# A two-layer transformer kernel on one core: another opening, score banks of a group from different row bands, and another pace table

## The chip, the core and the metric

The kernel runs on one core of a Trainium2 chip. The core has TensorE (PE; its weight loads are listed as PEld), VectorE (DVE), ScalarE (ACT), GpSimd (POOL) and SyncE (SP, which issues the DMAs). The metric is device time in microseconds of one execution.

## The reference

```python
x = A_x                                   # 2048 tokens, 448 features, bf16
x = x + attention(layernorm(x), wqkv, wo) # 16 heads of 28, softmax over all 2048 keys
x = x + mlp(layernorm(x), w1, b1, w2, b2) # relu(h)**2, hidden size 1792
x = x + attention(layernorm(x), wqkv, wo) # the same weights again
x = x + mlp(layernorm(x), w1, b1, w2, b2)
```

With `attention`: `softmax(q k^T / sqrt(28)) v`, all heads side by side, times `wo`. The layernorm has no weights. The exponential of 2 x 16 x 2048 x 2048 scores is the largest single piece of work.

## The kernel before, in words

**Units.** A head takes 32 rows of TensorE (28 used), so four heads, a group, stand side by side in K and Q as four row bands (`hh`, 0 to 3) of 32 rows; there are 4 groups. A unit is one head's scores of 512 columns, that is one PSUM bank: two key tiles of 128 against a block of 256 queries (four key tiles against 128 queries for the last blocks). Each layer has 1024 units. A pass is (layer, query block, group, range of key tiles); its units come as key step by key step, four heads each.

**Score groups.** `s_stream` takes the units three at a time, into one of two score buffers `sc` of three banks (matmuls at L978, one row band per unit, `tile_position`). `e_stream` has ScalarE compute the exponential of a whole score group in one instruction (L1003), three or two banks wide, into one of 12 buffers `pt`. Where it is two, VectorE takes the third bank (`a_unit`, `a_rest`): it computes the exponential as powers of two with a polynomial in three instructions (L1068, L1089, L1109), and POOL does a fourth (L1092). There are 683 score groups, numbered by `gi`. Which units VectorE takes is decided by `apart`: not if VectorE's load or backlog is over thresholds (`BUSY`, `TB`, `LOW`, `TB2`), unless `gi` stands in `FORCE`, and never if it stands in `SKIP`. `apart` may choose a unit of the next pass instead (`LAG`), and only there does it look for a row band that the group hasn't got yet. `LEAD` and `STOP` keep it out of the first 15 groups and the last 80 units.

**Other streams.** `p_stream` multiplies the probabilities by V (L1173) and copies or adds partial sums (L1199, L1201); `norm_pair` and `norm_turn` divide by the row sums; `chain` does the output projection, the second layernorm, the MLP (L693 for all dense matmuls) and, in layer 0, the layernorm and K, Q, V of layer 1 for that block. `first_block` does layernorm (L546, L551, L656, L608) and K, Q, V (L716, L712 or L710, L744) of each block of 256 tokens in layer 0, as the loads of x land. `heat` puts in matmuls with no use where TensorE's load is low, and a score group may be computed twice (`MORE`) for the same reason. `wprep` copies the projection weights into heads of 32 rows (L493 on ScalarE, L495 on VectorE).

**Order.** Everything is put in an order at build time by a planner. It keeps a clock for each engine and an expected duration for each operation, and issues next the stream whose operation can start first, by priority where two can. Most of the numbers at the top of the file are priorities, thresholds and expected durations of this planner; `PACE` overwrites them when the score group number reaches the key. The chip then executes the instructions of each engine strictly in the planned order.

**Opening.** Layer 0 can't wait until K exists for all tokens, so the first two query blocks go over the keys in pieces: `OPENING` lists (query block, first key tile, last key tile), and partial sums are kept between the pieces. In block 0, `GS0` says which groups of heads are projected together: `((0, 2), (2, 2))` is two groups at a time, first group and count. `GATE` holds back the layernorm of a block until a score group or a projection has been issued. `FIRSTS`, `VP`, `QP`, `VG`, `VG1`, `VP2` are priorities and gates of the first blocks and their V; `WQA` says from which head on the copies of wq go to VectorE.

The lines by which the order of the opening is set, and the choice of the units of a group:

```python
OPENING = ((0, 0, 2), (0, 2, 4), (1, 0, 4), (0, 4, 8), (1, 4, 8), (0, 8, 12), (0, 12, 16), (1, 8, 16))
GATE = (None, None, ('s', 2), ('Q', 0, 2, 0), ('s', 8), ('s', 10), ('s', 8), ('s', 14))
FIRSTS = (4, 1.5)
GS0 = ((0, 2), (2, 2))
...
js = ahead(3)
us = [units[j] for j in js]
```

Of the kernel before, what the change touches and what calls it, by code (L numbers as in the profile page):

```python
# [52 lines left out]
MARGIN = 1.5  # L53
# [9 lines left out]
ONE = 1  # L63
# [18 lines left out]
KEEP = 6  # L82
LAG = 12
LEAD = 15
LAST = 690
BUSY = 0.97
TB = 2.2
TB2 = 0.9
SPAN = 15
# [4 lines left out]
MORE = 1  # L94
# [3 lines left out]
LASTP = 3.2  # L98
HOLD = 6
HOLD1 = 7  # L100
SOON = 0
NHP = 2
THIRD = 1
NL = 0
# [14 lines left out]
TADD = 2  # L119
THALF = 0  # L120
CUTS = (0, 10, 16)
CH = 4.0
MMC = 0.46
EFIRST = 0
VGAP = 0.0
QP = 8.0
FORCE = (24, 30, 31, 58, 59, 129, 192, 193, 272, 289, 295, 320, 324, 326, 376, 384, 419, 425, 474, 475, 476, 479, 481,
        523, 525, 536, 537, 539, 553, 555, 557, 568, 570, 573, 579, 581, 582, 583, 600, 605)
SKIP = (57, 132, 133, 135, 195, 198, 199, 273, 278, 288, 292, 379, 381, 383, 385, 386, 390, 427, 429, 430, 472, 478,
        480, 485, 487, 521, 522, 543, 575, 603)  # L130
PACE = {
    0: {'ASIDE': 2.0, 'BUSY': 0.97, 'CH': 4.0, 'CHUNK': 2, 'C_PRIO': 1.6, 'EPRIO': 2.5, 'FAR': 9, 'HOLD': 6,
         'KEEP': 6, 'L1N': 5.6, 'LAG': 12, 'LASTP': 3.2, 'LEAD': 15, 'MARGIN': 1.5, 'NEAR': 6, 'PRE': 0.5,
         'QP': 8.0, 'SOON': 0, 'SPAN': 15, 'TB': 2.2, 'TB2': 0.9, 'V_AGE': 5, 'V_LAST': 2.5, 'V_LATE': 4.6,
         'V_PAST': 2},
    8: {'V_LATE': 3.5, 'EPRIO': 8},
    16: {'EPRIO': 2.5},
    40: {'LAG': 16},
    56: {'CHUNK': 1},
    72: {'EPRIO': 8, 'LEAD': 12, 'SOON': 1.0},  # L140
    96: {'LAG': 12, 'KEEP': 4},
    112: {'V_LAST': 3.5},
    120: {'BUSY': 0.995, 'ASIDE': 1.0},
    136: {'BUSY': 0.985, 'CHUNK': 3},
    144: {'BUSY': 0.995, 'CHUNK': 1},
    264: {'HOLD': 5},
    272: {'HOLD': 6, 'LAG': 8, 'TB': 2.6, 'V_LAST': 1.8},
    280: {'LAG': 12, 'TB': 2.2, 'V_LAST': 3.5, 'PRE': 0.8},
    288: {'PRE': 0.5},
    296: {'PRE': 0.3},  # L150
    320: {'C_PRIO': 2.6},
    328: {'CHUNK': 3},
    336: {'CHUNK': 1},
    344: {'EPRIO': 2.5, 'L1N': 5.0},
    360: {'SPAN': 11},
    376: {'LASTP': 2.6, 'SPAN': 15},
    384: {'TB': 3.0, 'TB2': 1.4},
    392: {'TB': 2.2, 'TB2': 0.9},
    400: {'MARGIN': -1, 'V_LATE': 4.0, 'SPAN': 20},
    408: {'C_PRIO': 1.6},  # L160
    416: {'FAR': 17, 'SOON': 0},
    432: {'LAG': 8},
    440: {'LAG': 12, 'CH': 5, 'EPRIO': 4},
    496: {'LASTP': 3.2},
    536: {'NEAR': 4},
    560: {'FAR': 9, 'QP': 5},
    576: {'V_PAST': 5, 'TB': 3.0},
    584: {'V_PAST': 0, 'TB': 2.2, 'CH': 3.3, 'V_AGE': 6},
    600: {'BUSY': 0.97, 'SOON': 1.0},
    608: {'BUSY': 0.995, 'SOON': 0},  # L170
    632: {'TB': 1.8, 'C_PRIO': 4.2},
    640: {'FAR': 17, 'CHUNK': 2},
    648: {'LAG': 5},
    656: {'LAG': 12},
}


# [134 lines left out]
def kernel(  # L312
# [43 lines left out]
    pl = Planner()  # L356
# [457 lines left out]

    for qb, lo, hi in OPENING:
        add_passes(0, [qb], (lo, hi))
# [10 lines left out]
    units = []  # L827
# [5 lines left out]
    ends_at = {pi: i for i, (pi, *_) in enumerate(units)}  # L833
# [4 lines left out]
    at = [0]  # L838

    taken = set()  # L840
# [24 lines left out]

    def apart(i, now, us, soon=SOON):

        if len(units) - i < STOP or not LEAD <= len(gbuf) <= LAST:
            return None
        l, qb = passes[units[i][0]][:2]  # L870
        if sum(r.when() is not None and r.when() <= now + soon for r in sets_of(units[i])) <= (0 if soon else pending[0]):
            return None
        j = i
        if i + LAG > ends_at[units[i][0]]:
            j = ends_at[units[i][0]] + 1
            while j in taken:
                j += 1
            if j >= len(units):
                return None
            rows = {u[3] for u in us}  # L880
# [24 lines left out]

    def needs(unit):
        pi, kb, r, hh = unit
        l, qb, g, *_ = passes[pi]
        t0, nt = blocks[l][qb]
        return [("K", l, g, kb + i) for i in range(r)] + [("Q", l, g, t0 + i) for i in range(nt)]  # L910

    def s_stream():
        while at[0] < len(units):
            gi = len(gbuf)
            globals().update(PACE.get(gi, {}))
            js = ahead(3)
            us = [units[j] for j in js]
            gbuf.append({"n": len(us)})

            def fn(e, gi=gi, us=us, js=js):  # L920
# [5 lines left out]
                def next_at(j):  # L926
                    at[0] = j
                    rest = ahead(1)
                    at[0] = rest[0] if rest else len(units)
                    return rest  # L930
                own, j = True, None
                if OWN3 and bank_free(o.start) and next_at(js[-1] + 1):
                    j = apart(at[0], o.start, us)
                if j is None and len(us) == 3 and THIRD:
                    own = False
                    next_at(js[1] + 1)
                    j = apart(at[0], o.start, us[:2], 0.0)
                if j is None:
                    next_at(js[-1] + 1)
                else:  # L940
                    if not own:
                        us, ks = us[:2], ks[:2]
                        gbuf[gi]["n"] = 2
                    us, ks = us + [units[j]], ks + [3]
                    taken.add(j)
# [3 lines left out]
                    next_at(at[0])  # L949
# [16 lines left out]
                again = 0  # L966
                if short > 0 and gi > 0:
                    last = ("e" in gbuf[gi - 1] and gbuf[gi - 1]["e"].end) or pl.clock["ACT"] + 1.35
                    again = max(0, min(MORE, int(min(o.room, last - LAT["PE"] - 0.05 - o.end) / 0.22)))
                o.more = 0.22 * again  # L970
                for i in list(range(4)) * (again + 1):
                    for k, (pi, kb, r, hh) in enumerate(us):
                        if i >= r:
# [3 lines left out]
                        rows = slice(DHP * hh, DHP * hh + DHP)  # L977
# [4 lines left out]
            o = gbuf[gi]["s"] = Op("PE", 0.234, fn,  # L982
                                   deps=list({d for u in us for d in needs(u)}), acq=R_sc, mode="row", sets=("s", gi))
# [492 lines left out]
```

## Time and profile before

| | us |
|---|---|
| three runs | 842.81, 844.40, 844.43 |
| median | 844.4 |
| the profiled execution: its own time | 842.93 |
| its span | 841.1 |
| ScalarE busy | 825.3 |
| VectorE busy | 795.8 |
| TensorE busy | 790.1 |
| first exponential starts | 10.63 |

The span runs from the first to the last instruction of the program; some 1.8 us of the execution lie around it. The granted TensorE clock is full speed throughout. A row of a group reads: line, engine, operation, output and input tiles, shapes, count, then busy us, mean ns of one, and the engine's idle time just before with what ended it. A row of a timeline reads: start us, length us, engine, line, operation, count, and in brackets the engine's idle time before it. Exponentials overlap at their ends, so that the mean duration of one is longer than the distance from start to start.

### The profile page before, as it was taken

What the parts mean: (1) busy time and instruction counts of PE and PEld (TensorE: products, weight loads), DVE (VectorE), ACT (ScalarE), POOL (GpSimd) and SP (SyncE); (2) the same over time, 40 slices, a digit from 0 to 9 for tenths busy, and PEclk for the clock granted to TensorE, in tenths of its full rate; (3) what the DMA queues carried; (4) which work ended last, traced back from release to release, by engine and by line L of the source; (5) the groups of instructions that cost most, each with busy time, mean ns of one, the idle gap of its engine ahead of it and who ended that gap; (6) DMA issues with size and microseconds to landing.
All of it is one profiled execution on the core that took longest, in us unless ns stands there. A gap on an engine that the chain in (4) does not pass through costs nothing.

```text
span 841.1 us, 27889 instructions
## 1 busy us (share of the span) xinstructions
PE 790.1 (94%) x11972; PEld 423.3 (50%) x11972; DVE 795.8 (95%) x1548; ACT 825.3 (98%) x699; POOL 220.3 (26%) x338
## 2 busy tenths in 40 slices
PE   8999999999999999999999999889999999999997
PEld 4455545454545554455554544444444544545655
DVE  7999999999999999999999999999999999999954
ACT  8999999999999999999999999999999999999994
POOL 3211222323232222322222223232324133232200
PEclk9999999999999999999999999999999999999999
DMA  9200100000000000000000000011100000000000
GB/s 251 68 3 2 29 17 15 15 15 16 15 2 16 15 15 16 14 3 15 2 3 2 2 3 2 15 28 28 34 8 20 21 20 26 13 21 15 21 14 13
DMA packets 32312, 17.93 MB, mean 21 GB/s; under 512 B 17786, under 2 KB 31739, under 8 KB 32188
## 3 DMA queue, kind: packets, MB, share of 16 engines
q1 hardware_dynamic: 32188, 16.16, 7.0%
q8 instruction: 93, 1.52, 0.8%
q14 instruction: 31, 0.25, 0.1%
HBM read 13.87 MB, written 2.06 MB: 19 GB/s over the span
## 4 chain that ended last, share of the span: by engine, by line
ACT 47%; PE 34%; DVE 10%; issue 8%; POOL 0%; DMA 0%; ACTq 0%; DVEq 0%; POOLq 0%
ACT pt L1003 47%; PE mt L693 14%; PE sc L978 12%; PE oT L1173 7%; DVE v_e L1089 1%; DVE v_i L1068 1%; PE sc L693 1%; PE mt L1425 1%; DVE K_sb L1068 1%; DVE r L1369 1%; DVE V_sb L1089 1%; DVE oTn L1300 0%; DVE V_sb L1068 0%; DVE pt L1109 0%; DVE x_sb L1309 0%
## 5 line engine op out<-in xcount | busy, mean ns | idle before, releaser
L1003 ACT ACTIVATE pt<-sc 128x1536 bf16<-128x1536 f32 (+1 forms) x683 | 814.6, 1469 | 2.0 <-PE sc L978 1.9
L978 PE MATMUL sc<-Q_sb,K_sb 32*128 32x256 bf16 (+1 forms) x5038 | 298.1, 265 | 40.8 <-ACT pt L1003 35.0
L978 PEld LDWEIGHTS <-K_sb 32*128 32x128 bf16 x5038 | 128.7, 92 | 217.0 <-issue 171.4
L1092 POOL TENSOR_SCALAR v_i<-v_i 128x512 int32<-128x512 int16 x129 | 96.3, 746 | 255.1 <-DVE v_e L1089 252.4
L1173 PE MATMUL oT<-pt,V_sb 128*32 128x256 bf16 (+1 forms) x4070 | 150.6, 268 | 1.1 <-DVE K_sb L608 0.8
L693 PE MATMUL mt<-xnT,w 128*128 128x256 bf16 (+1 forms) x912 | 120.3, 270 | 0.5 <-DVE xnT L608 0.3
L1173 PEld LDWEIGHTS <-V_sb 128*32 128x32 bf16 x4352 | 92.1, 96 | 45.7 <-issue 43.1
L693 PEld LDWEIGHTS <-w 128*128 128x128 bf16 x952 | 77.7, 98 | 36.4 <-issue 28.5
L1068 DVE TENSOR_SCALAR v_i<-sc 128x512 int32<-128x512 f32 x129 | 88.1, 685 | 4.2 <-PE sc L978 3.5
L1089 DVE SCALAR_TENSOR_TENSOR v_e<-v_i 128x512 f32<-128x512 uint16 x129 | 89.5, 704 | 0.2
L1092 POOL TENSOR_SCALAR K_sb<-K_sb 128x512 int32<-128x512 int16 x68 | 47.9, 704 | 131.8 <-DVE K_sb L1089 130.1
L1369 DVE TENSOR_SCALAR r<-mt 128x512 bf16<-128x512 f32 (+1 forms) x109 | 74.4, 683 | 4.2 <-PE mt L693 3.8
L693 PE MATMUL mt<-w,V_sb 128*128 128x448 bf16 x274 | 69.4, 355 | 0.0
L1092 POOL TENSOR_SCALAR V_sb<-V_sb 128x512 int32<-128x512 int16 x46 | 31.1, 676 | 104.8 <-DVE V_sb L1089 103.9
L1068 DVE TENSOR_SCALAR K_sb<-sc 128x512 int32<-128x512 f32 x68 | 46.5, 685 | 1.7 <-PE sc L978 1.3
L1089 DVE SCALAR_TENSOR_TENSOR K_sb<-K_sb 128x512 f32<-128x512 uint16 x68 | 46.1, 688 | 0.2
L573 POOL TENSOR_TENSOR ve<-mv,eps_t 128x2 f32<-128x2 f32 (+1 forms) x34 | 14.1, 416 | 114.6 <-DVE mv L551 114.2
L1309 DVE TENSOR_TENSOR x_sb<-x_sb,mt 128x448 bf16<-128x448 bf16 x61 | 37.2, 611 | 7.1 <-PE mt L693 7.1
L546 DVE BATCH_NORM_STATS2 st<-x_sb 128x6 f32<-128x448 bf16 x62 | 38.0, 616 | 0.9 <-DMA x_sb<-in_A_x_dram 0.7
L693 PEld LDWEIGHTS <-V_sb 128*128 128x128 bf16 x302 | 24.5, 97 | 25.4 <-issue 12.2
L1109 DVE SCALAR_TENSOR_TENSOR pt<-v_e,v_i 128x512 bf16<-128x512 f32 x52 | 35.7, 689 | 0.2 <-POOL v_i L1092 0.2
L1068 DVE TENSOR_SCALAR V_sb<-sc 128x512 int32<-128x512 f32 x46 | 31.5, 685 | 1.6 <-PE sc L978 1.6
(114 smaller groups left out, 857.4 us busy)
## 6 DMA issues: line engine op xcount, KB each, us to landing
rec<-scr SPq DMA_DIRECT2D x54, 128.0 KB
x_sb<-in_A_x_dram SPq DMA_DIRECT2D x8, 224.0 KB
out_dram<-x_sb SPq DMA_DIRECT2D x15, 112.0 KB
w<-in_B_w_dram SPq DMA_DIRECT2D x1, 1568.0 KB
w<-in_B_w_dram SPq DMA_DIRECT2D x1, 1344.0 KB
dn<-oT_sb SPq DMA_DIRECT2D x54, 4.0 KB
V_sb<-in_A_wqkv_dram SPq DMA_DIRECT2D x4, 168.0 KB
scr<-dn SPq DMA_DIRECT2D x27, 8.0 KB
```

The costliest lines, as they stand in the source:

```text
L546: nc.vector.bn_stats(out=box["st"][:, :], in_=x_sb[:, t0 + j, :] if src is None else src())
L573: nc.gpsimd.tensor_tensor(out=ve[:, a:b], in0=mv[0][:, a:b, 1], in1=eps_t[:, a:b], op=ALU.add)
L693: nc.tensor.matmul(box["t"][:, c0:c0 + n], lhsT=lhsT() if callable(lhsT) else lhsT, rhs=rhs, start=a, stop=b)
L978: nc.tensor.matmul(dst[k][:, i * nt * P:(i + 1) * nt * P], lhsT=K_sb[l][rows, g, (kb + i) * P:(kb + i + 1) * P], rhs=Q_sb[rows, g, t0 * P: ...
L1003: t = nc.scalar.activation(out=pt[:, 0:n], in_=gbuf[gi]["sc"][:, 0:n], func=AF.Exp, scale=float(np.log(2.0)) * 2.0 ** -FRAC)
L1068: t = nc.vector.tensor_scalar(out=box["i"], in0=two(src), scalar1=EXP_BIAS, scalar2=EXP_LOW, op0=ALU.add, op1=ALU.max)
L1089: nc.vector.scalar_tensor_tensor(out=box["h"], in0=box["f"], scalar=lin, in1=box["f"], op0=ALU.add, op1=ALU.mult)
L1092: (nc.vector if e == "DVE" else nc.gpsimd).tensor_scalar(out=box["e"], in0=box["n"], scalar1=2.0 ** 22, scalar2=EXP_BASE, op0=ALU.mult, op ...
L1109: nc.vector.scalar_tensor_tensor(out=box["two"](pd), in0=box["h"], scalar=low, in1=box["e"].bitcast(DT.float32), op0=ALU.add, op1=ALU.mult)
L1173: nc.tensor.matmul(box["t"][DHP * hh:DHP * hh + DHP, 0:n], lhsT=V_sb[l][:, kb + i, 4 * g + hh, :], rhs=p[:, c0:c0 + n], start=begin and kb ...
L1309: nc.vector.tensor_tensor(out=x_sb[:, tb, lo:hi], in0=x_sb[:, tb, lo:hi], in1=t[:, 0:hi - lo], op=ALU.add)
L1369: nc.vector.tensor_scalar(out=r[:, 0:w], in0=t[:, 0:w], scalar1=0.0, scalar2=None, op0=ALU.max)
```

## The change

The new version of the file does four things.

- In the opening, block 0 is projected by single groups of heads, two passes change places with two others, the gates, priorities and the place of V differ, the copies of wq all go to ScalarE (`WQA = 16`), and the statistics of block 1 wait for the transposed x of block 0 (`XT = 1`).
- `ahead` fills a group of three with units of different row bands: it looks up to `AHEADS` = 4 units further, takes a unit out of turn only if its K and Q are there already, and falls back to the next ones in turn. `use` keeps the list of units that were taken out of turn. In `apart` the search for another row band (`AHEADV` = 6) holds within a pass too.
- The planner expects 0.2 us more for a score group with a row band twice (`deep`).
- `FORCE`, `SKIP`, `PACE` and several defaults have new values.

```diff
-EPRIO = 2.5
+EPRIO = 4
-WQA = 8
+WQA = 16
-L0N = 7.0
+L0N = 5
-XT = 0
+XT = 1
-OPENING = ((0, 0, 2), (0, 2, 4), (1, 0, 4), (0, 4, 8), (1, 4, 8), (0, 8, 12), (0, 12, 16), (1, 8, 16))
+OPENING = ((0, 0, 2), (0, 2, 4), (1, 0, 4), (1, 4, 8), (0, 4, 8), (0, 8, 12), (1, 8, 16), (0, 12, 16))
-GATE = (None, None, ('s', 2), ('Q', 0, 2, 0), ('s', 8), ('s', 10), ('s', 8), ('s', 14))
+GATE = (None, None, ('Q', 0, 2, 0), ('Q', 0, 2, 0), None, None, ('s', 5), None)
-FIRST = 50
-V_FIRST = 9
+FIRST = 40
+V_FIRST = 7
+AHEADS = 4
+AHEADV = 6
-FIRSTS = (4, 1.5)
+FIRSTS = (4, 3)
-GS0 = ((0, 2), (2, 2))
+GS0 = ((0, 1), (1, 1), (2, 1), (3, 1))
-VP = 4.2
+VP = 8
-VG = 2
-VG1 = 5
-VP2 = 4.3
+VG = 3
+VG1 = 2
+VP2 = 3
-QP = 8.0
-FORCE = (24, 30, 31, 58, 59, 129, ...
-SKIP = (57, 132, 133, 135, 195, ...
+QP = 9
+FORCE = (21, 33, 34, 36, 74, 77, 79, 87, 109, 110, 130, 132, 157, 158, 159, 260, 416, 419, 448, 450, 451, 455, 536,
+        617, 620, 622, 623, 642, 643, 646)
+SKIP = (17, 20, 22, 24, 25, 26, 28, 31, 32, 35, 37, 39, 72, 73, 75, 78, 86, 131, 133, 134, 135, 155, 156, 258, 259,
+        417, 452, 454, 538, 540, 619, 621, 644, 647)
...
+    304: {'MORE': 3},
+    328: {'V_PAST': 5},
...
+    400: {'TB2': 2.2, 'MARGIN': 0.5, 'V_LAST': 3.5},
...
+    488: {'MORE': 1, 'BUSY': 1.01, 'V_LATE': 4.6},
+    552: {'MARGIN': 2.5, 'TB': 1.8},
...
-        j = i
-        if i + LAG > ends_at[units[i][0]]:
-            j = ends_at[units[i][0]] + 1
+        j, end = i, ends_at[units[i][0]] + 1
+        rows = {u[3] for u in us}
+        if i + LAG >= end:
+            j, end = end, len(units)
...
-            js = [k for k in range(j, j + 4) if k < len(units) and k not in taken and units[k][3] not in rows]
-            j = js[0] if js else j
+        js = [k for k in range(j, min(j + AHEADV, end)) if k not in taken and units[k][3] not in rows]
+        j = js[0] if js else j
...
     def ahead(n):
-        return [i for i in range(at[0], min(at[0] + n + len(taken), len(units))) if i not in taken][:n]
+        c = [i for i in range(at[0], min(at[0] + n + AHEADS + len(taken), len(units))) if i not in taken][:n + AHEADS]
+        out = []
+        for i in c:
+            if len(out) < n and units[i][3] not in {units[k][3] for k in out} and (i in c[:n] or all(pl.tok.get(d) is not None and pl.tok[d].end < pl.clock["PE"] for d in needs(units[i]))):
+                out.append(i)
+        return out + [i for i in c if i not in out][:n - len(out)]
+    def use(js):
+        taken.update(js)
+        while at[0] in taken:
+            taken.discard(at[0])
+            at[0] += 1
+        rest = [i for i in range(at[0], min(at[0] + 1 + len(taken), len(units))) if i not in taken]
+        return rest[0] if rest else len(units)
...
-                o.more = 0.22 * again
+                deep = max(sum(u[3] == w[3] for u in us) for w in us) - 1
+                o.more = 0.22 * again + 0.2 * deep * (again + 1)
```

More of the change, by code (lines that the diff above doesn't have):

```diff
@@ L100 @@
 HOLD1 = 7
-SOON = 0
+SOON = 1
 NHP = 2
@@ L125 @@
 VGAP = 0.0
-QP = 8.0
[L127 to L130, printed above, removed]
-PACE = {
[L132 to L142, printed above, removed]
-    120: {'BUSY': 0.995, 'ASIDE': 1.0},
[L144 to L174, printed above, removed]
@@ new lines @@
+QP = 9
[3 more added lines that the diff above has]
+        417, 452, 454, 538, 540, 619, 621, 644, 647)
+PACE = {
+    0: {'ASIDE': 2.0, 'BUSY': 0.97, 'CH': 4.0, 'C_PRIO': 1.6, 'EPRIO': 4, 'EV': 2.9, 'KEEP': 6, 'L0N': 5,
+         'L1N': 5.6, 'LAG': 12, 'MARGIN': 1.5, 'MORE': 1, 'NEAR': 2, 'QP': 9, 'SOON': 1, 'TB': 2.2, 'TB2':
+         0.9, 'V_AGE': 6, 'V_LAST': 2.5, 'V_LATE': 4.6, 'V_PAST': 2, 'V_PRIO': 8.5, 'V_WAIT': 5},
+    24: {'C_PRIO': 2.6},
+    32: {'C_PRIO': 1.6},
+    48: {'EPRIO': 1.5},
+    88: {'V_LATE': 4.0},
+    104: {'QP': 5},
+    112: {'QP': 9},
+    120: {'BUSY': 0.995, 'ASIDE': 1.0},
+    168: {'EV': 3.3, 'V_LAST': 1.8, 'V_WAIT': 3.5},
+    304: {'MORE': 3},
+    328: {'V_PAST': 5},
+    336: {'LAG': 5},
+    344: {'LAG': 12, 'EV': 1.5},
+    392: {'V_PAST': 2, 'V_LATE': 5.2},
+    400: {'TB2': 2.2, 'MARGIN': 0.5, 'V_LAST': 3.5},
+    416: {'MORE': 1, 'EPRIO': 4},
+    424: {'KEEP': 3, 'EV': 3.3},
+    432: {'V_PAST': 5, 'CH': 3.3},
+    440: {'MORE': 3, 'EPRIO': 2.5},
+    448: {'MORE': 1, 'EPRIO': 1.5, 'L1N': 5.8, 'KEEP': 6},
+    456: {'L1N': 5.6, 'KEEP': 3, 'EPRIO': 2.5},
+    480: {'MORE': 3},
+    488: {'MORE': 1, 'BUSY': 1.01, 'V_LATE': 4.6},
+    552: {'MARGIN': 2.5, 'TB': 1.8},
+    568: {'L0N': 8.4, 'V_LATE': 2.7},
+    576: {'L0N': 5, 'V_LATE': 4.6},
+    632: {'V_PAST': 0, 'V_PRIO': 3.5},
+    648: {'V_AGE': 3, 'SOON': 0},
+    656: {'V_AGE': 6, 'SOON': 1},
@@ L879, in apart @@
                 return None
-            rows = {u[3] for u in us}
-            js = [k for k in range(j, j + 4) if k < len(units) and k not in taken and units[k][3] not in rows]
-            j = js[0] if js else j
+        js = [k for k in range(j, min(j + AHEADV, end)) if k not in taken and units[k][3] not in rows]
+        j = js[0] if js else j
         if passes[units[j][0]][0] != passes[us[0][0]][0]:
@@ L924, in fn @@
                 ks = list(range(len(us)))
[L926 to L930, printed above, removed]
                 own, j = True, None
-                if OWN3 and bank_free(o.start) and next_at(js[-1] + 1):
-                    j = apart(at[0], o.start, us)
+                i = use(js[:2])
                 if j is None and len(us) == 3 and THIRD:
                     own = False
-                    next_at(js[1] + 1)
-                    j = apart(at[0], o.start, us[:2], 0.0)
+                    j = apart(i, o.start, us[:2], 0.0)
                 if j is None:
-                    next_at(js[-1] + 1)
+                    use(js[2:])
                 else:
@@ L944, in fn @@
                     us, ks = us + [units[j]], ks + [3]
-                    taken.add(j)
+                    use([j])
                     gbuf[gi]["in"] = not own and units[j][0] == us[0][0]
@@ L948, in fn @@
                     pending[0] += 1
-                    next_at(at[0])
                     if own:
```

2 lines of the change are left out of this document (1 added, 1 removed).

## The prediction

> **What bounds the kernel now.** I read the page's engine shares first, then the groups of instructions with shapes kept apart, then the busy time by stretches, then the opening in order of time.
>
> ```profile
> span 841.1 us, 27889 instructions
> ...
> PE 790.1 (94%) x11972; PEld 423.3 (50%) x11972; DVE 795.8 (95%) x1548; ACT 825.3 (98%) x699; POOL 220.3 (26%) x338
> ```
>
> Three engines are nearly full, and ScalarE (ACT) most of all. The next view says with what; behind the x stand the count, the busy us and the mean ns of one.
>
> ```profile
> L1003 ACT ACTIVATE pt<-sc 128x1536 bf16<-128x1536 f32 x439 | 644.6, 1621 | 1.9 <-PE sc L978 1.9
> L1003 ACT ACTIVATE pt<-sc 128x1024 bf16<-128x1024 f32 x244 | 278.6, 1195 | 0.2
> L1089 DVE SCALAR_TENSOR_TENSOR v_e<-v_i 128x512 f32<-128x512 uint16 x129 | 89.5, 704 | 0.2
> L1068 DVE TENSOR_SCALAR v_i<-sc 128x512 int32<-128x512 f32 x129 | 88.1, 685 | 4.2 <-PE sc L978 3.5
> L1109 DVE SCALAR_TENSOR_TENSOR pt<-v_e,v_i 128x512 bf16<-128x512 f32 x52 | 35.7, 689 | 0.2 <-POOL v_i L1092 0.2
> L1199 DVE COPY K_sb<-oT 128x256 f32<-128x256 f32 x20 | 8.4, 418 | 0.3 <-PE oT L1173 0.3
> ```
>
> There are 683 exponentials, three score banks wide or two. A bank more costs 1621 - 1195 = 426 ns of ScalarE. The banks add to 439 x 3 + 244 x 2 = 1805; the 2048 units of 512 columns leave 243 that VectorE (DVE) computes with three instructions each, 685 + 704 + 689 = 2.08 us (the fourth, on POOL, is beside them). The trade that sets the time is therefore: one unit more on VectorE is 0.43 us less on ScalarE, if VectorE has 2.08 us to spare. Where it has, and when ScalarE runs, shows in these stretches (length, then busy us of PE, PEld, DVE, ACT, POOL):
>
> ```profile
> 0.00:10.60 10.60, 8.69 (x59) 4.91 (x59) 6.88 (x29) 7.61 (x10) 4.76 (x13) 1.00 0.80 207
> 10.60:25.00 14.40, 13.66 (x156) 7.60 (x153) 13.27 (x32) 13.44 (x10) 3.01 (x8) 1.00 1.05 304
> 40.00:800.00 760.00, 718.06 (x10821) 379.45 (x10822) 741.65 (x1403) 759.51 (x643) 206.77 (x305) 1.00 0.05 14
> 240.00:320.00 80.00, 76.77 (x1133) 40.71 (x1134) 79.03 (x152) 80.00 (x69) 22.23 (x34) 1.00 0.05 13
> 320.00:400.00 80.00, 74.97 (x1094) 38.76 (x1083) 75.35 (x144) 79.97 (x68) 22.23 (x35) 1.00 0.05 12
> 400.00:480.00 80.00, 76.53 (x1127) 40.70 (x1121) 78.28 (x149) 80.00 (x69) 19.31 (x34) 1.00 0.01 2
> 826.60:841.20 14.60, 10.88 (x133) 8.00 (x131) 6.36 (x17) 3.19 (x7) 0.75 (x2) 1.00 0.06 17
> ```
>
> So the span is 10.6 us ahead of the first exponential, 816.0 us of exponentials, 14.5 us of last dense work. Between 40 and 800 us VectorE idles 18.4 us. The cadence inside the 816 us comes from a late stretch in order of time (start, length):
>
> ```profile
> 798.45 28.17 ACT L1003 ACTIVATE pt<-sc 128x1536 bf16<-128x1536 f32 x21
> ```
>
> 28.17 / 21 is 1.34 us for three banks, so 0.91 for two (less 0.43): 439 x 1.34 + 244 x 0.91 = 810. Some 6 us of the 816 are lost to exponentials that start late, and the rate has short waits of its own in it.
>
> **The change part by part.** First the opening. The rows that lead to the first exponential and to the only long gap behind it:
>
> ```profile
> 7.34 0.38 DVE L495 COPY wq<-V_sb 128x896 bf16<-128x896 bf16 x1
> 7.47 1.03 PE L693 MATMUL sc<-xnT,wk 128*128 128x256 bf16 x8
> 7.51 0.93 ACT L493 COPY wk<-V_sb 128x896 bf16<-128x896 bf16 x1
> 8.35 1.04 PE L693 MATMUL mt<-xnT,wq 128*128 128x256 bf16 x8
> 8.55 0.69 DVE L716 CAST K_sb<-sc 128x512 bf16<-128x512 f32 x1 [0.82 <-PE sc L693]
> 9.15 0.62 DVE L546 BATCH_NORM_STATS2 st<-x_sb 128x6 f32<-128x448 bf16 x1
> 9.42 0.60 ACT L710 ACTIVATE Q_sb<-mt 128x512 bf16<-128x512 f32 x1 [0.97 <-PE mt L693]
> 9.80 0.18 DVE L551 BATCH_NORM_AGGREGATE mv<-st 128x2 f32<-128x6 f32 x1
> 10.19 0.61 PE L978 MATMUL sc<-Q_sb,K_sb 32*128 32x256 bf16 x12
> 10.63 10.94 ACT L1003 ACTIVATE pt<-sc 128x1536 bf16<-128x1536 f32 x8 [0.61 <-PE sc L978]
> 21.66 0.69 DVE L712 TENSOR_SCALAR Q_sb<-mt 128x512 bf16<-128x512 f32 x1 [0.18 <-PE mt L693]
> 22.06 0.61 PE L978 MATMUL sc<-Q_sb,K_sb 32*128 32x256 bf16 x12
> 22.50 2.79 ACT L1003 ACTIVATE pt<-sc 128x1536 bf16<-128x1536 f32 x2 [0.93 <-PE sc L978]
> ```
>
> *Single groups* (GS0). Eight K matmuls for two groups take 7.47 to 8.50, eight Q matmuls to 9.39, then 0.60 of Q copy. With one group, four K matmuls end near 7.99 and four Q matmuls near 8.51. The copies are half as wide, 0.42 (the L1199 row has that shape), so K is ready near 8.46 and Q near 8.95. From the end of Q's copy, 9.42 + 0.60 = 10.02, to the exponential at 10.63 it is 0.61 now; the same behind 8.95 gives 9.56. The first exponential comes 1.07 us earlier. Ends: nothing, if the copies line up behind other work, and 1.6 us, if K and Q evacuate on two engines and scores aren't repeated first. I take 1.07.
>
> *wq on ScalarE* (WQA). The 0.38 copy leaves VectorE, a copy of 0.93 (the wk row has its shape) goes behind 8.44 on ScalarE and ends at 9.37, ahead of 9.56: nothing. If Q's copy queues behind it on ScalarE, the first exponential slips to 9.37 + 0.38 + 0.61 = 10.36. The half-width copies cost VectorE 4 x 2 x 0.42 against 4 x 0.69, 0.6 us more, partly ScalarE's; that lies beside exponentials.
>
> *Gates, priorities of values, XT.* The gap of 0.93 at 21.6 us ends when Q of block 1 is copied at 21.66. Ahead of it VectorE did layernorm of blocks 2 and 3 and the V copies (0.62 each), which are needed later. After the change block 2 and 3 wait for Q of group 2, and V comes at a lower priority; but blocks 4, 5 and 7 lose their gates. An exponential that starts 1.07 earlier also needs that Q 1.07 earlier. I take half of the gap as recovered, 0.5. Ends: the whole 0.9 recovered; or lost, below.
>
> *Pass order.* The eight opening passes are the same ones; (1,4,8) changes places with (0,4,8) and (1,8,16) with (0,12,16). Same matmuls, same partial sums. Block 1 is now finished first and the first dense chain starts 32 units, about 14 us, later; its output is first needed by layer 1, hundreds of us on: nothing. It costs if that leaves VectorE with idle time early and too much later.
>
> *More alternation.* Four more projection groups alternate with score matmuls. Price of a switch:
>
> ```profile
> 17.81 0.39 PE L978 MATMUL sc<-Q_sb,K_sb 32*128 32x256 bf16 x6
> 18.14 1.31 PE L693 MATMUL mt<-wv,xnT 128*128 128x448 bf16 x6
> 22.60 0.40 PE L1173 MATMUL oT<-pt,V_sb 128*32 128x256 bf16 x8
> ```
>
> Twelve score matmuls hold PE 22.60 - 22.06 = 0.54, six 18.14 - 17.81 = 0.33; six cost 0.21, so a switch costs 0.12. Four more in and out are 8 x 0.12 = 1.0 us of PE by 25 us, where PE idles 1.9 + 0.7 us. I take it as hidden; bound 0 to 1.0. The Trainium skill, TensorEngine Tiling (Array Packing), section Tiling Modes, says that changing the tiling mode drains TensorE; by that rule, with PE as the path of the opening, the 1.0 comes off the gain and the sum is 1.0 us higher. The trace agrees on a price at each switch (0.12 us).
>
> *Row bands.* When two units of a group sit in one 32-row band, their matmuls queue:
>
> ```profile
> 109.53 0.61 PE L978 MATMUL sc<-Q_sb,K_sb 32*128 32x256 bf16 x6
> ...
> 394.20 0.40 PE L978 MATMUL sc<-Q_sb,K_sb 32*128 32x256 bf16 x6
> 395.52 0.61 PE L978 MATMUL sc<-Q_sb,K_sb 32*128 32x256 bf16 x6
> 746.23 0.61 PE L978 MATMUL sc<-Q_sb,K_sb 32*128 32x256 bf16 x6
> ```
>
> 0.21 us more than normal. There are twelve such groups of six (109.53 the first, 746.23 the last) and five doubled ones, 17 x 0.21 = 3.6 us of PE. PE runs just ahead of ScalarE, so a late group delays an exponential by part of that. I take half, 1.8; ends 3.6 and nothing. Taking a unit out of turn (at most four ahead) could hold score or probability buffers longer; PE order is what it is made of, and I price it at nothing, because the buffers are a ring of 12 against a look-ahead of two groups.
>
> *Pace table, FORCE, SKIP.* No instruction gets a new price; they decide which units VectorE takes and when dense work runs. The bound is VectorE's idle time: 18.4 / 2.08 = 9 units, 3.8 us. From the other side, thresholds that hold back 12 units cost 5.1 us. Between the two the nearest row is the stretch 320 to 400, which idles 4.65 where its neighbours idle 0.97 and 1.72: levelled, 3.3 us, 1.6 units, 0.7 us. I take 0.7. STOP is unchanged, so the last 80 units and the 14.5 us tail stay.
>
> Sum: 1.07 + 0.5 + 1.8 + 0.7 = 4.1 us. The profiled execution took 842.93 (span 841.1), so 838.8 on its footing. The three runs shown are 842.81, 844.40 and 844.43, median 844.4, on average 0.95 above the profiled one; that gives 839.8. A difference under 0.2% (1.7 us) can't be told from none.
>
> **The rivals.**
> *A, slower: the opening clogs.* Blocks 4, 5 and 7 have no gate any more, so their layernorm is ready for VectorE as soon as x lands. Its other two steps are
>
> ```profile
> 14.30 0.68 DVE L608 COPY xnT<-tp 128x1024 bf16<-128x1024 bf16 x1
> 17.70 0.39 DVE L656 TENSOR_SCALAR xn<-x_sb,mv,rstd 128x448 bf16<-128x448 bf16 x1
> ```
>
> With statistics that is 6 x (0.62 + 0.18 + 0.39) + 3 x 0.68 = 9.2 us. If all of it runs between the copies of K and Q, the gap at 21.6 grows by as much, and the 0.5 isn't won. For: VectorE is 92% busy from 10.6 to 25, with 1.1 us to spare. Against: they stand behind the copies in priority and get VectorE only when a copy isn't ready. Sum 839.8 + 0.5 + 9.2 = 849.5. It ends slower (over 846.1) from 6.3 us lost.
>
> *B, slower: fewer units on VectorE.* SKIP holds 34 numbers, 12 of them under 40. With 18 units fewer, 7.7 us, and without the 0.7, it is 842.93 - 3.37 + 7.7 + 0.95 = 848.2; it ends slower from 14 fewer. For: two nearly full engines share the units, and one threshold moves many. Against: at 14 fewer VectorE's idle time would be 18.4 + 14 x 2.08 = 47.5 us, more than twice what it is.
>
> *C, nothing happens.* The earlier start returns whole in the gap at 21.6, which waits for work that isn't shortened, and the groups with one band twice turn out to have had the time: only the pace is left, 842.93 - 0.7 + 0.95 = 843.2. For: PE and VectorE, not ScalarE, set the pace up to 22 us. Against: ScalarE has no idle time before the gap that could be called cover.
> *D, much faster.* All 9 units, 3.1 more than taken, and 3.0 of the 3.7 us that the sum still leaves lost between exponentials: 839.8 - 3.1 - 3.0 = 833.7. For: the idle time is there. Against: the neighbours of the one loose stretch idle 0.97 and 1.72 in 80.
>
> **How the numbers follow.** Forecast 0.50 (its own range 836.5 to 842.5), D 0.11, C 0.11, A 0.12, B 0.16. Faster: forecast and D, 0.61; same: C and part of A, 0.13; slower 0.26. The range reaches from D to B and leaves out the far half of both: 833.5 to 848.
>
> **What would show it.** First exponential near 9.6 us. No gap over 0.5 us in the first 25. No groups of six matmuls at 0.61 but a few. Two-bank exponentials between 240 and 253 in place of 244: this count, times 0.43, is the term that can overturn the rest; below 231 the forecast is wrong. VectorE's idle time from 320 to 400 under 2 us. Last dense stage still near 14.5 us.

## The result

The changed kernel takes 841.67 us (median of 11 executions, 841.64 to 842.14); the kernel before, beside it on the same chip, 844.3 us (842.81 to 844.92). The medians lie 2.6 us apart, 0.3%; the ratio of the executions is put at 0.9979, 95% interval 0.9971 to 0.9986, so 0.2% faster. The forecast was 839.8, 4.6 us under the 844.4 shown; it is 2.6 us under the median beside it, and part of that comes from something the forecast didn't have at all.

The two profiled executions differ by less than the medians: 842.93 to 841.64, 1.3 us, spans 841.1 to 839.9. The medians differ by 2.6 because six of before's 11 executions stood at 844.3 to 844.9 and five at 842.8 to 843.2, while all 11 of the changed kernel lie within 0.5 us. What the upper six are is shown with the last experiments; until then the 1.3 us are to be explained.

The page of the changed kernel, engine shares:

```profile
span 839.9 us, 27898 instructions
...
PE 789.1 (94%) x11983; PEld 421.8 (50%) x11983; DVE 791.4 (94%) x1546; ACT 825.6 (98%) x699; POOL 214.9 (26%) x336
```

Its groups of instructions with shapes kept apart (count, then busy us, mean ns of one); the line numbers of the exponentials and score matmuls are now L1000 and L975:

```profile
L1000 ACT ACTIVATE pt<-sc 128x1536 bf16<-128x1536 f32 x441 | 656.8, 1650 | 0.9 <-PE sc L975 0.9
L1000 ACT ACTIVATE pt<-sc 128x1024 bf16<-128x1024 f32 x242 | 286.8, 1234 | 0.1
```

441 three-bank exponentials against 439, 242 two-bank ones against 244: VectorE has two units fewer, not two more.

Its ScalarE in order of time, in the opening and at the end:

```profile
8.76 0.93 ACT L483 COPY wq<-V_sb 128x896 bf16<-128x896 bf16 x1
9.60 6.80 ACT L1000 ACTIVATE pt<-sc 128x1536 bf16<-128x1536 f32 x5
17.34 9.51 ACT L1000 ACTIVATE pt<-sc 128x1536 bf16<-128x1536 f32 x7 [0.94 <-PE sc L975]
...
825.27 0.63 ACT L1371 ACTIVATE V_sb<-r 128x512 bf16<-128x512 bf16 x1
```

The first exponential starts at 9.60 (10.63 before), right behind wq's copy, which ends at 9.69; ScalarE has no idle time between them. The gap didn't go: before it was 0.93 us ahead of the ninth exponential, now it is 0.94 ahead of the sixth. The sixth starts at 17.34; five cadences behind 10.63 it would start at 17.33 in the kernel before, and by the trace it does at 17.43: there the lead of 1.03 is all but gone. The ninth starts three cadences on, near 21.36, against 22.50 before, and there the opening has won 1.14 us. Three later executions with the same opening (after_again, pin_m6, stop40) start the first exponential at 9.38 to 9.53 and the sixth at 17.38 to 17.52, with 0.94 of idle time ahead of it in each; so a single start in the opening is good to about 0.2 us, the gap to 0.01.

The busy times by stretches (length, then PE, PEld, DVE, ACT, POOL):

```profile
10.60:25.00 14.40, 14.19 (x157) 7.95 (x153) 14.06 (x37) 13.46 (x11) 3.89 (x10) 1.00 1.06 296
40.00:800.00 760.00, 716.79 (x10843) 378.81 (x10841) 738.72 (x1402) 759.94 (x643) 201.48 (x302) 1.00 0.05 14
320.00:400.00 80.00, 76.24 (x1115) 40.04 (x1114) 77.86 (x152) 80.00 (x68) 21.27 (x36) 1.00 0.05 12
825.30:839.90 14.60, 10.88 (x133) 8.00 (x131) 6.35 (x17) 3.19 (x7) 0.75 (x2) 1.00 0.06 17
```

The loose stretch 320 to 400 was tightened (VectorE idles 2.1 us there in place of 4.65), but over 40 to 800 VectorE idles 21.3 us against 18.4. The last dense stage is the same 14.6 us. So the 1.3 us are: 1.1 won in the opening, 2 x 0.43 = 0.9 lost with two units, and a rest of 1.1, which can only be exponentials that start less late elsewhere. The experiments take these apart.

### The profile page after: what moved, and what is told of

It reads as the page before. It is cut to its first block, busy times and chain, and to the rows that moved or that the text cites. A ratio compares the mean times of both kernels' runs of the same rounds, so it can differ in the third digit from the quotient of the medians.

```text
span 839.9 us, 27898 instructions
## 1 busy us (share of the span) xinstructions
PE 789.1 (94%) x11983; PEld 421.8 (50%) x11983; DVE 791.4 (94%) x1546; ACT 825.6 (98%) x699; POOL 214.9 (26%) x336
## 4 chain that ended last, share of the span: by engine, by line
ACT 51%; PE 30%; DVE 11%; issue 8%; POOL 0%; ACTq 0%; DVEq 0%; POOLq 0%
ACT pt L1000 51%; PE mt L683 11%; PE sc L975 10%; PE oT L1170 6%; DVE r L1366 1%; DVE v_i L1065 1%; DVE pt L1106 1%; DVE K_sb L1065 1%; DVE v_e L1086 1%; PE mt L1422 1%; PE sc L683 1%; DVE K_sb L1086 1%; PE mt L422 1%; DVE xnT L598 1%; PE tp L586 1%
## 5 line engine op out<-in xcount | busy, mean ns | idle before, releaser
L1000 ACT ACTIVATE pt<-sc 128x1536 bf16<-128x1536 f32 (+1 forms) x683 | 814.7, 1503 | 1.0 <-PE sc L975 0.9
L975 PE MATMUL sc<-Q_sb,K_sb 32*128 32x256 bf16 (+1 forms) x5042 | 294.3, 265 | 41.2 <-ACT pt L1000 35.3
L975 PEld LDWEIGHTS <-K_sb 32*128 32x128 bf16 x5042 | 126.6, 92 | 218.4 <-issue 166.8
L1089 POOL TENSOR_SCALAR v_i<-v_i 128x512 int32<-128x512 int16 x127 | 92.0, 724 | 257.6 <-DVE v_e L1086 246.5
L1170 PE MATMUL oT<-pt,V_sb 128*32 128x256 bf16 (+1 forms) x4068 | 148.6, 268 | 0.4
L1086 DVE SCALAR_TENSOR_TENSOR v_e<-v_i 128x512 f32<-128x512 uint16 x127 | 86.8, 691 | 0.3
L563 POOL TENSOR_TENSOR ve<-mv,eps_t 128x2 f32<-128x2 f32 (+1 forms) x34 | 12.3, 360 | 91.5 <-DVE mv L541 90.7
L1106 DVE SCALAR_TENSOR_TENSOR pt<-v_e,v_i 128x512 bf16<-128x512 f32 x49 | 33.5, 684 | 1.6 <-POOL v_i L1089 1.6
```

Source lines behind the costliest of these rows:

```text
L563: nc.gpsimd.tensor_tensor(out=ve[:, a:b], in0=mv[0][:, a:b, 1], in1=eps_t[:, a:b], op=ALU.add)
L975: nc.tensor.matmul(dst[k][:, i * nt * P:(i + 1) * nt * P], lhsT=K_sb[l][rows, g, (kb + i) * P:(kb + i + 1) * P], rhs=Q_sb[rows, g, t0 * P: ...
L1000: t = nc.scalar.activation(out=pt[:, 0:n], in_=gbuf[gi]["sc"][:, 0:n], func=AF.Exp, scale=float(np.log(2.0)) * 2.0 ** -FRAC)
L1086: nc.vector.scalar_tensor_tensor(out=box["h"], in0=box["f"], scalar=lin, in1=box["f"], op0=ALU.add, op1=ALU.mult)
L1089: (nc.vector if e == "DVE" else nc.gpsimd).tensor_scalar(out=box["e"], in0=box["n"], scalar1=2.0 ** 22, scalar2=EXP_BASE, op0=ALU.mult, op ...
L1106: nc.vector.scalar_tensor_tensor(out=box["two"](pd), in0=box["h"], scalar=low, in1=box["e"].bitcast(DT.float32), op0=ALU.add, op1=ALU.mult)
```

## The experiments

**Row bands alone, put in and taken out.** Two kernels: the one before with the new choice of units and its own tables, and the changed one with the old choice.

```diff
 # rows_only: the changed file with before's OPENING, GS0, GATE, XT, WQA, FIRSTS, VP, VG, VG1, VP2,
 # EPRIO, L0N, FIRST, V_FIRST, SOON, QP, FORCE, SKIP, PACE
+    ahead(), use(), apart(), deep of the change
 # rows_off: the file before with the changed kernel's values of the same constants
-    ahead(), use(), apart(), deep of the change
```

> The kernel before with the new choice of units by row band alone (new ahead, use, apart and deep; opening, FORCE, SKIP and PACE as before). 243 units stay on VectorE, and of the 16 score groups with a row band twice none is left. Theory 1 (a late score group delays an exponential by about half of its 0.21 us, as predicted): 1.8 us faster in the profiled execution, and the exponentials' late starts shrink by as much. Theory 2 (the exponential is seldom late by it, since PE usually runs ahead): under 0.6 us. In both the first exponential stays at 10.63.

> The changed kernel with the old choice of units (rows not looked at, the old ahead and apart), opening and tables as after. 241 units stay on VectorE, 16 score groups have a row band twice again. Theory 1: 1.8 us slower than the changed kernel (span 841.7). Theory 2: under 0.6 us slower (span under 840.5). First exponential 9.6 in both.

rows_only took 842.48 us (842.28 to 843.07), span 840.8, ratio to before 0.9986 (0.9977 to 0.9995). rows_off took 842.24 (842.01 to 842.46), span 840.6. (Of the 21 executions of the kernel before beside them five stood at 844.5 or more; the other 16 have a median of 843.2, 0.7 above rows_only.) TensorE of rows_only in order of time, at the place that the prediction quoted at 395.52:

```profile
394.29 0.40 PE L987 MATMUL sc<-Q_sb,K_sb 32*128 32x256 bf16 x6
...
395.61 0.39 PE L987 MATMUL sc<-Q_sb,K_sb 32*128 32x256 bf16 x6
```

The group that took 0.61 takes 0.39: the mechanism is as predicted, but its worth isn't. The spans differ by 0.3 us between before and rows_only, 0.7 between rows_off and the changed kernel, in place of 1.8. Theory 2 holds on one side and is a little short on the other. A late score group costs ScalarE 0.3 to 0.7 / 17, some 0.02 to 0.04 us each, a tenth or a fifth of its 0.21, not half. That PE mostly runs ahead by more than that is the likely reason: in the kernel before, ScalarE idles only 2.1 us in all ahead of its exponentials. rows_only keeps the 243 units of the kernel before and rows_off has the 241 of the changed one, so it is not the new choice by row bands that takes two units from VectorE.

**Opening alone, tables alone.**

```diff
 # open_only: the file before with
+OPENING, GS0, GATE, XT, WQA, FIRSTS, VP, VG, VG1, VP2 of the change
 # pace_only: the file before with
+EPRIO, L0N, FIRST, V_FIRST, SOON, QP, FORCE, SKIP, PACE of the change
```

> The kernel before with the new opening alone (OPENING, GS0, GATE, XT, WQA, FIRSTS, VP, VG, VG1, VP2); rows, FORCE, SKIP and PACE as before. Theory 1 (the terms add): first exponential at 9.6 and the whole about 1.0 us faster, 842 us. Theory 2 (FORCE, SKIP and PACE go by the number of the score group, so a shifted opening makes them hit other work): first exponential at 9.6, but late starts later on grow by more than the 1.0 us won, and it is slower than before, by 5 us or more.

> The kernel before with the new EPRIO, L0N, FIRST, V_FIRST, SOON, QP, FORCE, SKIP and PACE alone; opening and rows as before. Theory 1 (the terms add): first exponential at 10.63, 241 units on VectorE, within 1 us of before. Theory 2 (the table only fits its own opening): slower than before by 5 us or more, from late starts and a longer last dense stage, with about as many units on VectorE.

open_only took 853.04 us (851.51 to 855.80), ratio 1.0117 (1.0098 to 1.0135); pace_only 851.3 (850.39 to 852.11), ratio 1.0092 (1.0078 to 1.0106). Each is some 7 to 10 us slower than the 843.2 of the kernel before, and together they are faster: rows_off, which has both and not the row bands, took 842.24. ScalarE of open_only in the opening:

```profile
9.64 7.05 ACT L1003 ACTIVATE pt<-sc 128x1536 bf16<-128x1536 f32 x5 [0.30 <-PE sc L978]
17.65 6.82 ACT L1003 ACTIVATE pt<-sc 128x1536 bf16<-128x1536 f32 x5 [0.95 <-PE sc L978]
```

and its groups, to be set beside the quoted ones:

```profile
L1003 ACT ACTIVATE pt<-sc 128x1536 bf16<-128x1536 f32 x440 | 639.0, 1583 | 2.9 <-PE sc L978 2.4
L1003 ACT ACTIVATE pt<-sc 128x1024 bf16<-128x1024 f32 x243 | 270.6, 1156 | 5.8 <-PE sc L978 5.3 <-PE oT L1173 0.4
```

The first exponential is early as planned (9.64) and 243 two-bank exponentials mean nearly as many units on VectorE as before, so neither the start nor the number of units makes it slow. ScalarE waits for scores: 8.7 us of idle time before exponentials in place of 2.1. Some 1 us of that, and as much in pace_only, is no matter of the schedule: in both profiled executions the granted clock is at half for 3.4 us (at 119.7 and 781.9), and ScalarE waits 0.86 and 1.13 us there; the executions at full clock took 851.5 and 852.6, and 850.4 and 850.6. The last dense stage is longer too, 16.7 us here and 18.7 in pace_only:

```profile
835.00:851.70 16.70, 13.49 (x181) 10.68 (x179) 6.78 (x18) 5.61 (x11) 0.75 (x2) 1.00 0.07 23
```

```profile
831.50:850.20 18.70, 15.41 (x180) 11.30 (x179) 8.11 (x20) 4.34 (x8) 0.75 (x2) 1.00 0.08 26
```

FORCE, SKIP and PACE name score groups by number; with another opening the same numbers meet other work. Theory 2 holds in sign and size for both. Opening and tables have no price of their own that could be added up; of the parts tried alone only the row bands have. The tables weren't taken apart further, so which of their entries make the late starts isn't shown.

**The opening's two halves.** First single groups against two.

```diff
-GS0 = ((0, 1), (1, 1), (2, 1), (3, 1))
+GS0 = ((0, 2), (2, 2))
```

> The changed kernel with GS0 back at two groups of heads at a time; nothing else. If the earlier first exponential comes from single groups: it starts at 10.6 or later in place of 9.6. If it comes from the place of wq, V or the gates instead, it stays under 10. If the gap at exponential 5 is work on VectorE and PE that has to be done anyway, the gap shrinks by about what the first exponential loses, from 0.94 to under 0.5.

It took 844.24 us (one execution), span 842.5. ScalarE of gs0_two in order of time:

```profile
9.39 0.60 ACT L700 ACTIVATE Q_sb<-mt 128x512 bf16<-128x512 f32 x1
10.60 2.79 ACT L1000 ACTIVATE pt<-sc 128x1536 bf16<-128x1536 f32 x2 [0.61 <-PE sc L975]
13.69 4.17 ACT L1000 ACTIVATE pt<-sc 128x1536 bf16<-128x1536 f32 x3 [0.30 <-PE sc L975]
18.44 12.20 ACT L1000 ACTIVATE pt<-sc 128x1536 bf16<-128x1536 f32 x9 [0.58 <-PE sc L975]
```

Single groups make the 1.0 us, as expected. That the gap would shrink by as much was wrong: it is 0.58, with 0.30 ahead of the third exponential, 0.9 together, and the sixth exponential starts 1.10 later than with single groups (18.44 against 17.34). So what the sixth waits for comes later too when two groups are projected at a time; why wasn't followed. After that this kernel loses another 1.5 us (842.5 - 839.9 = 2.6 in all); its trace has waits of 0.74 and 0.93 us for scores at 41.8 and 84.8, which the changed kernel hasn't got.

Then the statistics that stand between block 1's steps.

```diff
-GATE = (None, None, ('Q', 0, 2, 0), ('Q', 0, 2, 0), None, None, ('s', 5), None)
+GATE = (None, None, ('K', 0, 0, 2), ('K', 0, 0, 2), None, None, ('s', 5), None)
```

> The changed kernel with the layernorm of blocks 2 and 3 held back until K of block 1 is projected (GATE[2] and GATE[3] wait for it in place of Q of group 2). If the statistics of blocks 2 and 3, which run between block 1's steps on VectorE at 13.3, 14.5 and 15.7, make the gap at exponential 5: it falls from 0.94 to under 0.5. If block 1's own chain (statistics, POOL, transposes, K) makes it: 0.8 to 1.0. Later score groups meet FORCE, SKIP and PACE at other work, so the whole is slower by some us in either case.

It took 856.1 us (one execution), span 854.3. VectorE of the changed kernel ahead of the gap:

```profile
13.33 0.62 DVE L536 BATCH_NORM_STATS2 st<-x_sb 128x6 f32<-128x448 bf16 x1
13.86 0.67 DVE L598 COPY xnT<-tp 128x1024 bf16<-128x1024 bf16 x1
...
14.54 0.59 DVE L536 BATCH_NORM_STATS2 st<-x_sb 128x6 f32<-128x448 bf16 x1
15.05 0.61 DVE L734 CAST V_sb<-mt 128x448 bf16<-128x448 f32 x1
...
15.66 0.59 DVE L536 BATCH_NORM_STATS2 st<-x_sb 128x6 f32<-128x448 bf16 x1
16.17 0.67 DVE L706 CAST K_sb<-mt 128x512 bf16<-128x512 f32 x1
```

and of gate_k, then its ScalarE:

```profile
13.77 0.69 DVE L598 COPY xnT<-tp 128x1024 bf16<-128x1024 bf16 x1 [0.17 <-PE tp L586]
14.60 0.62 DVE L734 CAST V_sb<-mt 128x448 bf16<-128x448 f32 x1
15.14 0.62 DVE L536 BATCH_NORM_STATS2 st<-x_sb 128x6 f32<-128x448 bf16 x1
15.91 0.69 DVE L706 CAST K_sb<-mt 128x512 bf16<-128x512 f32 x1
```

```profile
17.09 4.27 ACT L1000 ACTIVATE pt<-sc 128x1536 bf16<-128x1536 f32 x3 [0.61 <-PE sc L975]
...
538.86 13.69 ACT L1000 ACTIVATE pt<-sc 128x1024 bf16<-128x1024 f32 x12 [7.74 <-PE sc L975]
```

Of the three statistics between 13.3 and 16.2 one is left; since blocks 2 and 3 are held back there, it must belong to a block without a gate. The idle time is 0.61, between the two expectations, where the four executions with the old gates have 0.94: the statistics of blocks 2 and 3 make 0.33 us of the gap. The way to K says the same. The statistics of block 1 start at 9.29 in gate_k and at 9.21 in the changed kernel, K's copy at 15.91 and 16.17, so K comes 0.34 sooner behind them. The other 0.61 is put down to block 1's own chain; no run shortened that chain. The price comes 500 us later: ScalarE waits 7.74 us for one score group at 538.9. Which step made that wait was not followed.

**The price of a unit.** Two kernels with another number of units on VectorE, the first with the changed kernel's decisions written out.

```diff
 # pin_m6
-FORCE = (21, 33, ...), SKIP = (17, 20, ...)
+FORCE = frozenset(the 241 groups with a unit on VectorE, less the last six: 641, 642, 643, 649, 651, 653)
+SKIP = frozenset(range(700)) - FORCE
 # stop40
-STOP = 80
+STOP = 40
```

> The changed kernel with its own decisions written out in FORCE and SKIP, but the last six units that VectorE took (score groups 639 to 653) left to ScalarE: 235 units in place of 241. By the price of the prediction (0.43 us a unit): 2.6 us slower, all of it in the exponentials. If VectorE's relief at the end speeds up the last dense stage: less, near nothing.

> The changed kernel with STOP = 40 in place of 80, so that VectorE may take units until 40 before the end, where it idles over half of the time: 247 units in place of 241. By the price of a unit alone: exponentials end 2.6 us earlier, and the whole is 2.6 us faster. Rival: VectorE then holds up the dense work of the last blocks, the last dense stage gets longer than 14.5 us by more than that, and the kernel is the same or slower.

pin_m6 took 845.82 us (845.77 to 846.41), ratio to before 1.0034 (1.0021 to 1.0046), span 844.0; stop40 846.39 (844.77 to 847.54), ratio 1.0039 (1.0026 to 1.0053), span 843.1. Stretches of pin_m6 (its exponentials end at 827.9), then of stop40 (823.2):

```profile
827.90:844.00 16.10, 11.46 (x121) 8.84 (x120) 6.27 (x17) 1.79 (x3) 0.75 (x2) 0.89 0.05 15
```

```profile
823.20:843.10 19.90, 16.61 (x186) 11.79 (x184) 8.26 (x20) 4.45 (x8) 0.75 (x2) 0.98 0.08 25
```

pin_m6: the exponentials end 827.9 - 825.3 = 2.6 us later for six units, 0.43 each, the price of the prediction. The other 1.5 us are in the last stage, where the granted clock is 0.89 (at half from 834.1 to 837.5). stop40 has 247 units on VectorE; its exponentials end 2.1 us earlier, and its last dense stage takes 19.9 us in place of 14.6, with PE busy for 16.6 of them in place of 10.9. The rival holds: 5.3 us lost for 2.1 won, since dense work of the last blocks that was done beside the exponentials is now left for the end. (Its profiled execution is one of the two at 844.8 to 844.9; the three at 846.4 to 847.5 have a mean clock of 0.996 to 0.997.) VectorE's idle time at the end is not free, and the two units that the new table gave up are worth 0.9 us.

**The executions of 844.4.** The kernel before, unchanged, twice more.

> The kernel before, unchanged, to see what lies between its executions of about 842.9 and those of about 844.4 (11 runs of the first measurement: five at 842.8 to 843.2, six at 844.3 to 844.9). Theory 1 (a step in the granted clock): an execution of 844.4 shows a mean clock of 0.998, and if it is the profiled one, a stretch with the clock at half late in the kernel, with the last dense stage longer than 14.5 us by about 1.5 and the exponentials as in the first profile. Theory 2 (the opening's loads land later in some executions): the clock is 1.00 and the first exponential starts 1.5 us later.

> The same once more, for another profiled execution. Same expectations.

Both profiled executions are of the longer kind (844.4 in the second; span 842.6 and mean clock 0.998 in both). Of the ten executions of before_again six lie at 842.87 to 843.13 with a clock of 1.00 and four at 844.35 to 844.53 with 0.998. Stretches of before_again; behind the five engines stand the granted clock, the DMA share and GB/s:

```profile
592.00:594.00 2.00, 1.45 (x24) 0.90 (x23) 2.00 (x4) 2.00 (x3) 1.21 (x3) 1.00 0.27 91
594.00:596.00 2.00, 1.48 (x28) 1.00 (x27) 2.00 (x5) 2.00 (x3) 0.66 (x2) 1.00 0.09 20
596.00:599.50 3.50, 3.50 (x68) 1.81 (x56) 2.27 (x4) 2.47 (x3) 1.68 (x2) 0.51 0.02 5
599.50:603.00 3.50, 3.50 (x41) 1.19 (x35) 2.86 (x6) 3.15 (x3) 0.00 (x0) 1.00 0.02 1
```

and its TensorE and ScalarE in order of time at that place:

```profile
593.89 0.40 PE L978 MATMUL sc<-Q_sb,K_sb 32*128 32x256 bf16 x6 [0.55 <-ACT pt L1003]
594.81 1.03 PE L978 MATMUL sc<-Q_sb,K_sb 32*128 32x256 bf16 x12 [0.52 <-ACT pt L1003]
...
597.75 0.61 PE L978 MATMUL sc<-Q_sb,K_sb 32*128 32x256 bf16 x6
```

```profile
598.47 1.02 ACT L1003 ACTIVATE pt<-sc 128x1024 bf16<-128x1024 f32 x1 [1.03 <-PE sc L978]
599.86 1.45 ACT L1003 ACTIVATE pt<-sc 128x1536 bf16<-128x1536 f32 x1 [0.36 <-PE sc L978]
```

TensorE has only score matmuls for 3 us, between waits for a score buffer, and then runs 3.4 us at half clock; a score group takes 0.61 in place of 0.39, and ScalarE loses 1.03 + 0.36 us. That is nearly the whole difference: up to there the exponentials stand where they stood in the first profile (within 0.04 us), behind it all are 1.47 us later. Theory 1 of a clock step holds, but at another place than expected: not in the last stage, but at 596 (from 596.09 to 599.50 here, from 595.66 to 599.08 in before_again2). The Trainium skill, TensorE: Matmul & The Clock Gate, Part 1 (The HAM clock gate), describes such a step: the clock goes to half after an idle window of about 3.4 us, and the window runs free, so that the same kernel meets it at another phase in each execution. The trace agrees with the length (3.41 us at 0.5), but the stretch before it was not idle: PE was busy for 1.45 + 1.48 of the 4 us ahead of it, most of it with score matmuls of 32 rows. Nor does the busy time alone single the place out: in the same execution PE is busy for 2.33 us between 592.7 and 596.1, and for just as much between 559.6 and 563.0, where the clock stays full. The two stretches differ in what PE does: near 560 a good part is matmuls of all 128 rows (L1173 and L1425). Whether that decides isn't shown.

To test it, those waits were filled with score matmuls that are computed again, and the changed kernel was run beside it.

```diff
-                for i in list(range(4)) * (again + 1):
+                fill = 2 * (gi in (489, 490))
+                for i in list(range(4)) * (again + 1 + fill):
```

> The kernel before with 24 more score matmuls (score groups 489 and 490 are computed four and three times over in place of two and one), put where PE waits twice for 0.5 us near 593 us, ahead of the place where the clock was at half for 3.4 us in two executions. Theory 1 (those idle stretches, when they fall into one window of the clock's regulation, make the step): no execution near 844.4 any more, all near 842.9, and the median falls where some of before's executions stand at 844.4. Theory 2 (the step has another cause): a share of executions near 844.4 as in before. In both the undisturbed time stays at 842.9, since PE only fills idle time.

> The changed kernel, unchanged, beside it on the same chip. If the step in the clock is before's alone: all executions within 0.6 us of 841.7, and against those of before_fill the difference is 1.3 us (the difference of the undisturbed profiles), not the 2.6 us of the first medians.

before_fill took 843.03 to 844.13 in 11 executions (median 843.21), all with a clock of 1.00; before beside it had four of 21 at 844.31 to 844.65, all with 0.998, and 17 at 842.84 to 843.32. after_again: 841.62 to 841.94, median 841.8, all with 1.00, ratio 0.9982 (0.9973 to 0.9991). Stretches of before_fill:

```profile
592.00:594.00 2.00, 1.89 (x37) 1.29 (x38) 1.70 (x4) 1.95 (x3) 1.24 (x3) 1.00 0.27 90
594.00:596.00 2.00, 1.76 (x35) 1.29 (x32) 2.00 (x5) 2.00 (x2) 0.37 (x1) 1.00 0.09 21
```

No execution of before_fill shows the step (with four in 21 as the share, 11 without one would come by chance one time in ten: 17/21 to the 11th power is 0.10; over all runs of before the executions at 844.3 or more are 22 of 86, 0.04). So the waits are the likely cause, and not a proven one. If they are, 32-row matmuls were enough to fill them. It pays 0.1 to 0.2 us for the extra matmuls, so its median isn't below before's. rows_only, rows_off and the changed kernel show none in 11, 11 and 22 executions; what keeps them clear of it wasn't traced. The changed kernel's difference to before_fill is 843.21 - 841.8 = 1.4 us, and to the 17 executions of before without the step (median 843.0) 1.2, as expected of the undisturbed profiles. So of the 2.6 us between the first medians about 1.3 are the work of the schedule and the other 1.3 the step in the clock. That more than half of before's executions had it in that first set is read from their times, 844.3 and more; their clocks weren't recorded.

## Why the prediction was wrong

*First exponential at 9.56:* measured 9.60. Right, by the mechanism named; gs0_two puts it back to 10.60. That it fits to 0.04 is luck: Q's copy ended at 8.85, 0.1 earlier than forecast, and the exponential then stood behind wq's copy. The other executions of the same opening have 9.38 to 9.53.

*Half of the gap recovered, 0.5:* this step failed, and the wait was misread. The prediction has the gap end when Q of block 1 is copied at 21.66. That copy ends at 21.66 + 0.69 = 22.35, but the ninth exponential's scores start at 22.06. They stood behind the copy of block 1's K and behind 12 matmuls for its Q on TensorE:

```profile
20.59 1.54 PE L693 MATMUL mt<-xnT,wq 128*128 128x256 bf16 x12
20.79 0.69 DVE L716 CAST K_sb<-mt 128x512 bf16<-128x512 f32 x1
```

In the changed kernel it is K of block 1 again, for the first two groups of heads, three exponentials earlier:

```profile
16.90 0.33 PEld L975 LDWEIGHTS <-K_sb 32*128 32x128 bf16 x11 [0.25 <-DVE K_sb L706]
```

The gap is 0.94 in place of 0.93. With the first exponential the opening won 1.14 at the ninth exponential in place of 1.57. gate_k shows a part of what holds it: 0.33 us are the statistics of blocks 2 and 3, which the new gates leave there. The rest is, by elimination, block 1's own chain on POOL, TensorE and VectorE, which starts no earlier than before (its statistics at 9.21, before at 9.15).

*wq on ScalarE, pass order, alternation at nothing:* the wq copy ends at 9.69 in place of 9.37, and the first exponential starts right behind it. It may hold it by 0.1 to 0.2 us; at the sixth, which waits for K, nothing of that is left. Alternation: PE is busy 14.19 of 14.40 from 10.6 to 25, 0.53 more than before; up to the ninth exponential ScalarE has no idle time but that one gap. Pass order alone wasn't tried.

*Row bands, 1.8:* mechanism right (0.61 becomes 0.39), term mis-sized: 0.3 to 0.7. I took half of TensorE's delay as ScalarE's; it is a tenth to a fifth, most likely because scores are ready ahead of ScalarE in most places. The view of waits had 35.0 us of TensorE waiting for ScalarE at L978 in the kernel before, which speaks for it; I didn't weigh it.

*Pace table, +1.6 units, 0.7:* the step that failed by the most, and in sign. The loose stretch was tightened as I took it to be, but elsewhere VectorE was left more idle (21.3 us in place of 18.4), and the units are 241, not 245: 0.9 lost in place of 0.7 won, 1.6 us of the difference. The price of 0.43 a unit is right (pin_m6). That idle time of VectorE could be filled with units was taken as given; stop40, which gave it six more near the end, lost. Why the new tables leave more of it idle between 40 and 800 us wasn't followed.

*Sum:* 1.1 + 0.3 to 0.7 - 0.9 + a rest of 0.4 to 0.8 = 1.3, against 4.1. The rest is what is left over: fewer late starts under the new tables, which no run shows by themselves. And the addition itself was wrong as a method: open_only and pace_only are 7 to 10 us slower alone, so that these two terms belong to one plan and have no worth apart.

*The footing:* I added 0.95 for the distance of the three runs to the profiled one, as if it were spread. It is a step in the clock that no execution of the changed kernel showed, so nothing was to be added: on the profiled execution's footing the forecast is 838.8, and 4.1 us stand against 1.3.

*Rivals:* A didn't come: ahead of the gap VectorE does statistics of blocks 2 and 3, which are gated. B came in part: two units fewer, not 14. C came in part too: at the sixth exponential the earlier start was back in the gap, and most score groups with a band twice had the time; but by the ninth 1.1 us of the opening stayed won. Nothing of D came.

## What to carry to other kernels

A schedule whose tables go by instruction number has to be searched as a whole: the opening or the tables alone, put into the other version, said nothing of their worth, and cost 1% here. Price a delay on a busy feeder by how far it runs ahead, not by its length, and idle time on a helper engine by what stands behind it. If the executions of one kernel fall in two heaps, look at the granted clock of each before adding their mean to a forecast.

## What the hardware showed that was not expected

In two traced executions of the kernel before, the granted clock of TensorE falls to half for 3.41 us at 596 us, after 3 us in which it had only 32-row score matmuls and two waits of 0.5 us; each time it costs 1.47 us. By their times, about a quarter of all its executions had such a step (22 of 86, at 844.3 or more; of the 75 whose clock is on record, the 16 among them show a mean of 0.998 and the others 1.00). The other traced execution passes the place at full clock with the same instructions. With 24 repeated score matmuls in the two waits there was no step in 11 executions; the changed kernel has none in 22, although nothing in it was made for that. A step of the same length stands in the profiled executions of open_only (119.7), pace_only (781.9) and pin_m6 (834.1, in the last stage, where it costs 1.5 us); all six executions of pin_m6 have a mean clock of 0.998.
